# Token-ordered Strassen sums, weight splits in pieces, input sums on GpSimd and moved down products in a two-layer attention and SwiGLU kernel

## The chip, the cores and the metric

The kernel runs on one core of a Trainium2 chip. The metric is the device time of one execution in microseconds (us), as the median of several runs. A row of the profile such as "PE bank L335" names an engine (PE = TensorE, DVE = VectorE, ACT = ScalarE, POOL = GpSimd, SP = the queue that issues DMAs), the tile written and the line of the kernel.

## What is computed

Two layers, each an attention block with one key and value head and a SwiGLU block, over 2048 tokens of width 448, all in float32:

```python
def _A_ref(x, wq, wk, wv, wo):          # B, S, D, H = 1, 2048, 448, 16
    q = (x @ wq) in 16 heads of 28;  k = x @ wk;  v = x @ wv
    p = softmax(q k^T * 28 ** -0.5)
    return (p v, heads joined) @ wo
def _B_ref(x, w_gate, w_up, w_down):    # F = 1792
    return (silu(x @ w_gate) * (x @ w_up)) @ w_down
for _ in range(2):
    x = x + _A_ref(layernorm(x), A_wq, A_wk, A_wv, A_wo)
    x = x + _B_ref(layernorm(x), B_w_gate, B_w_up, B_w_down)
```

## The kernel before

Every matrix product with weights is done on numbers split in two: a high part, rounded to the short float format that TensorE takes at full rate, and a low part, the rest. A product is then three matmuls (high x high, high x low, low x high), or fewer where a row half is shared. `split` (L138) makes the two parts on GpSimd: one TENSOR_SCALAR for the high part (L139), one TENSOR_TENSOR for the low one (L140).

**The feed-forward layer**, which the change touches, works on 4 token chunks c of 512 and 14 columns blocks fc of 128. Two column blocks are a group gi (7 groups). Groups 0 and 6 are done in *units* (`unit`, L1044), one per chunk and column block: gate and up products of the chunk in two banks of PSUM, in two halves of the contraction (two `side_by_side` calls), `Silu` on ScalarE (L1081), the product with up on VectorE (L1082), its high part `hh` on ScalarE (L1083), its low part `hl` on VectorE (L1086). The down products of a unit, two steps, are kept in a list `pend` and run in the next unit: the first step between that unit's halves, the second after them. After the last column block of a group the four banks of down products are added to the residual `xres` (`accumulate`, L977: two directly on VectorE, L985, two by a copy to a staging tile on ScalarE, L988, and an add on GpSimd, L989).

**Groups 1 to 5** are done by Strassen's method: per column block and pair of chunks (p = 0, 1) one *block* (`block`, L805), 20 blocks per layer. Its operands are sums: `T` of the input (made once per pair by `mix`, L777, 18 instructions of 128x512 each) and `S` of the weights (`sums`, L794, GpSimd). Its seven products go to banks x, y, z, w (steps A1 to A4, S0 to S5), and sums of these make gate and up of both chunks:

- `s1` copies x to SBUF (ScalarE, L850); `u2`, `w5`, `u3`, `C12`, `C22`, `C21` add banks and SBUF tiles (VectorE, L851 to L856). The SBUF tiles `u_, w_, v_, s_` are parts of the tile xn.
- `silB` (ScalarE, L857), `mulB` (VectorE, L859), `hhB` (L864), `hlB` (L868) make the hidden part of chunk b, and `silA` (L858, it reads bank x and so ends its use), `mulA` (L860), `hhA`, `hlA` that of chunk a.
- E1, E2 are the down products of chunk b, F1, F2 those of chunk a, each in four further banks. `fE`, `fF` and `fX` to `gZ` are tiny copies of one column per bank (`between`, "seen", L342) on ScalarE: TensorE writes a bank from its other row half only after them.
- Of E's and F's four banks, two are added to `xres` on VectorE (Ea0, Ea1, L882) and two copied to staging tiles on ScalarE (Ec2, Ec3, L877) and added on GpSimd (Ep2, Ep3, L884). There are **two** staging buffers, so Fc2 needs Ep2 to be done.

Within one column of a PSUM bank the tokens stand by the way they were turned: position n*4 + t holds token n of tile t. `in_turn` (L131) is the view of such a bank as (t, n), at a stride of four words; `by_tile` (L135) is the plain order. In before, the sums stay in the bank's order, and `silB`, `mulB` and `mulA` put them in token order when they read.

What sets the order of the work is the table `ORDER` (L765): each engine gets the steps in that order; a name with one dash belongs to the block before, with two dashes to the one before that. `w1` and `w2` are places for weight work: `w1` splits the weights of the column block after next (`parted`, L173) and makes their sums, ahead of Ep2 in GpSimd's queue; `x1`, `x2`, `x3` are places where `mix` instructions that are left over (`extra`) go. Nothing reorders it afterwards; an engine waits in order.

Blocks of a group in order j = 0 to 3: (p 0, A), (p 0, B), (p 1, A), (p 1, B). At j = 0 GpSimd splits the weights of block column B (from the second such group on); at j = 1 it makes sums and splits (groups 1 to 4; group 5 splits only); at j = 3 it makes sums.

`rest` (L1146) begins the feed-forward layer: the norm of chunk 3 (its copies of 64 columns of xn are L246, on GpSimd), then the sums of the first weights, then the groups. The transposes of chunk 3 (L285) stand in the unit (0, 2, 1).

Of the kernel before, what the change touches and what calls it, by code (L numbers as in the profile page):

```python
# [52 lines left out]
def forward(  # L53
# [292 lines left out]
    class Attention:  # L346
# [418 lines left out]
    ORDER = (  # L765
        "A1 C21- Fc2-- Fp2-- mulA- A2 fY fX Fa0-- Fa1-- A3 fZ fW Fc3-- Fp3-- A4 s1 hhA- u2 x1 E1- w1 w5 fE- u3 S0 "
        "hlA- x2 gY E2- Ea0- Ea1- x3 Ec2- Ep2- Ec3- Ep3- w2 S1 gX S2 gZ S3 gW S4 F1- C12 C22 silB mulB fF- S5 hhB hlB F2- silA"
    ).split()

    class FeedForward:  # L770
        def __init__(self, layer):
            self.layer, self.X, self.W, self.norms = layer, {}, {}, {}
            self.pend, self.soon, self.dn, self.flip, self.mid, self.left = [], [], {}, 0, {}, []
            self.blocks, self.extra = [], []
            self.nxt = Attention(1) if layer == 0 else None

        def mix(self, p):  # L777
# [4 lines left out]
            t = qraw  # L782
            tt = nc.vector.tensor_tensor
            fs = []
            for i, *terms in ((2, b1[0], b0[0], b0[1], b1[1]), (0, b0[0], a0[0], a0[1], b0[1]), (1, b1[0], t, None, b1[1]), (3, a1[0], t, None, a1[1])):
                fs.append(lambda x=terms[0], y=terms[1]: tt(t, x, y, ALU.subtract))  # L786
# [3 lines left out]
                fs.append(lambda i=i: nc.vector.tensor_copy(hi[i], t))  # L790
                fs.append(lambda i=i: tt(lo[i], t, hi[i], ALU.subtract))
            return fs
# [12 lines left out]
        def block(self, p, fc):  # L805
# [43 lines left out]
            tt = nc.vector.tensor_tensor  # L849
            o["s1"] = lambda: nc.scalar.copy(s_, x)  # L850
            o["u2"] = lambda: tt(u_, y, s_, ALU.add)  # L851
            o["w5"] = lambda: tt(w_, z, u_, ALU.add)
            o["u3"] = lambda: tt(v_, w, u_, ALU.add)
            o["C12"] = lambda: tt(w_, y, w_, ALU.add)  # L854
            o["C22"] = lambda: tt(v_, z, v_, ALU.add)
            o["C21"] = lambda: tt(u_, w, u_, ALU.add)  # L856
            o["silB"] = lambda: nc.scalar.activation(by_tile(s_), in_turn(w_), AF.Silu)  # L857
            o["silA"] = lambda: nc.scalar.activation(by_tile(sg), in_turn(x), AF.Silu)  # L858
            o["mulB"] = lambda: tt(by_tile(s_), in_turn(v_), by_tile(s_), ALU.mult)  # L859
            o["mulA"] = lambda: tt(by_tile(sg), in_turn(u_), by_tile(sg), ALU.mult)  # L860

# [4 lines left out]
            for k, raw, e, c in (("B", s_, "E", b), ("A", sg, "F", a)):  # L866
# [12 lines left out]
                def add(e, c, t):  # L879
                    r = xres[:, 4 * c + t, :]  # L880
                    if t < 2:
                        tt(r, d[t][:, 0:D], r, ALU.add)  # L882
# [6 lines left out]
                for t in range(4):  # L889
                    o[f"{e}{'aapp'[t]}{t}"] = lambda e=e, c=c, t=t: add(e, c, t)  # L890
                for t in (2, 3):
# [17 lines left out]
        def blocked(self, gi):  # L909
# [25 lines left out]
            for j, (p, fc) in enumerate((p, fc) for p in range(2) for fc in (A, B)):  # L935
                for n, k in (("x1", 2), ("x2", 1), ("x3", 1)):
                    jobs[j][n] = [self.extra.pop(0) for _ in range(min(k, len(self.extra)))]
                self.blocks.append(self.block(p, fc))
                self.run(jobs[j])
            if last:  # L940
                o = self.blocks[-1]
                self.blocks.append({})
                f = [o.pop(k) for k in ("F1", "fF", "F2")]
                self.run({})
                self.pend = [lambda: (f[0](), f[1]()), f[2], o["Fa0"], lambda: [o[k]() for k in ("Fc2", "Fp2", "Fa1", "Fc3", "Fp3")]]
                part(A + 3)

        def down(self, fs, fc, d, hh, hl, w=None):


            dh, dl = w or self.W[fc][2:]
            self.flip = 1 - self.flip
            one, two = ((0, 1), (2, 3)) if self.flip else ((2, 3), (0, 1))
# [90 lines left out]
        def unit(self, gi, c, n):  # L1044
# [92 lines left out]
        def verdict(self, last):  # L1137
# [6 lines left out]
            nc.vector.tensor_reduce(whole, row[0:1, 0:P], AX.X, ALU.min)  # L1144

        def rest(self, xb):  # L1146
            self.stage = xb.enter_context(tc.tile_pool(name=f"stage{self.layer}", bufs=2, reuse_waits="tile"))
# [6 lines left out]
            for c in (2, 3):  # L1154
                self.X[c] = xtile(self.xbp, self.xd[c])
            cut(self.norms[2], self.X[2])
# [5 lines left out]
            mixing = ExitStack()  # L1162
            if mixed:
                pool = mixing.enter_context(tc.tile_pool(name=f"mix{self.layer}", bufs=1, reuse_waits="tile"))
                self.S = [(q[:, 0, :], q[:, 1, :]) for q in qts]
                self.S.append((kd.rearrange("p g n -> p (g n)"), pool.tile([P, 512], F32R, name="sums")))
                self.apart = pool.tile([P, 512], F32, name="apart")
                self.T = [keys, [pool.tile([P, 2, 512], F32R, name=f"mixed{i}") for i in range(4)]]
                self.sums(FG, columns(FG))
                self.extra += self.mix(0)  # L1170
            for gi, fs in enumerate(groups):
# [9 lines left out]
                for c in range(NC) if gi not in mixed else ():  # L1181
                    for n in range(len(fs)):
                        if mixed and (gi, c, n) == (0, 3, 0):
                            self.extra += self.mix(1)
# [88 lines left out]
```

## Time and profile before

| what | us |
|---|---|
| median of 3 runs (2034.92 to 2038.86) | 2035.11 |
| the profiled execution's own time | 2036.95 |
| its span, first to last instruction | 2035.2 |
| TensorE busy in it | 1980.6 |
| feed-forward, layer 0: first stretch 592 to 667 / blocks 667 to 950 / end and next projection 950 to 1060, TensorE busy | 63.12 of 75 / 276.99 of 283 / 104.03 of 110 |
| feed-forward, layer 1: 1604 to 1678 / 1678 to 1960 / 1960 to 2035, TensorE busy | 62.96 of 74 / 276.24 of 282 / 65.88 of 75 |
| both attention layers, TensorE busy | 588.33 of 592, 543.11 of 544 |
| VectorE, ScalarE, GpSimd busy over the span | 1130.9, 1371.1, 729.2 |

Read the table by stages: TensorE has almost no pause in attention, and some 12 us in each first stretch, 6 in the blocks of each layer and 6 to 9 at each end. A row of the timeline gives start, duration (us), engine, line, operation, out<-in, size, and in brackets the idle time of that engine before it and what ended it. x2 at the end of a row are two instructions put together.

### The profile page before, as it was taken

How to read it: one execution, taken by the hardware profiler on the slowest of the kernel's cores; microseconds unless marked ns; L12 is line 12 of the kernel's file. 1: busy time of each engine (PE TensorE's matmuls, PEld its weight loads, DVE VectorE, ACT ScalarE, POOL GpSimd, SP SyncE). 2: the span in 40 equal slices, each digit the busy share in tenths (PEclk: the TensorE clock that was granted, in tenths of full speed). 3: DMA queues.
4: the chain of work that ended last, by engine and by line, in shares of the span. 5: the costliest groups of instructions: out<-in, count | busy, mean ns of one | idle time of the engine just before them, and what ended most of it. 6: DMA issues, size and time to landing. Idle time of an engine off the chain costs nothing. (4 is left out here: it accounts for less than half of the span.)

```text
span 2035.2 us, 45408 instructions
## 1 busy us (share of the span) xinstructions
PE 1980.6 (97%) x18267; PEld 1291.2 (63%) x18267; DVE 1130.9 (56%) x1805; ACT 1371.1 (67%) x2417; POOL 729.2 (36%) x772
## 2 busy tenths in 40 slices
PE   9999999999998999999999999999999979999998
PEld 7544545445477788888884444454444868888887
DVE  7443544545457676775564335445454577677753
ACT  4899898998932444444348998989989334444532
POOL 4222111124124566664342221212231245667540
PEclk9999999999998999999999999999999989999999
DMA  5111110212110011100131111102111100111102
GB/s 163 50 30 30 30 43 12 61 38 58 34 37 16 16 31 31 30 21 17 55 99 39 29 30 30 43 12 60 52 45 34 37 16 16 31 31 31 31 1 74
DMA packets 95510, 78.62 MB, mean 39 GB/s; under 512 B 23582, under 2 KB 78494, under 8 KB 95294
## 3 DMA queue, kind: packets, MB, share of 16 engines
q1 hardware_dynamic: 95006, 75.21, 13.2%
q8 instruction: 144, 2.36, 0.5%
q14 instruction: 72, 0.59, 0.1%
q10 hardware_dynamic: 288, 0.46, 0.1%
HBM read 56.11 MB, written 18.74 MB: 37 GB/s over the span
## 5 line engine op out<-in xcount | busy, mean ns | idle before, releaser
L659 PE MATMUL bank<-pt,vsb 128*32 128x512 f32 x4096 | 493.3, 598 | 0.3
L618 PE MATMUL bank<-qstack,keys 32*128 32x512 f32 x1536 | 484.6, 425 | 0.0
L618 PE MATMUL three<-qstack,keys 32*128 32x512 f32 x4608 | 459.8, 425 | 1.5 <-DVE vt L552 1.2
L618 PEld LDWEIGHTS three<-qstack,keys 32*128 32x128 f32 x4608 | 254.0, 182 | 295.3 <-ACT pt L631 181.1
L625 ACT ACTIVATE pt<-three 128x1536 f32<-128x1536 f32 x256 | 372.2, 1454 | 0.6 <-ACT pt L631 0.3
L631 ACT ACTIVATE pt<-three 128x1536 f32<-128x1536 f32 x256 | 372.1, 1454 | 0.0
L335 PE MATMUL bank<-xh,wgh 64*128 64x512 f32 x1248 | 330.7, 399 | 17.5 <-ACT sg L858 16.3
L335 PE MATMUL bank<-wdh,h 64*128 64x448 f32 x1776 | 315.8, 373 | 9.2 <-ACT h L864 6.6
L627 DVE COPY raw<-bank 128x512 f32<-128x512 f32 x256 | 177.4, 693 | 226.4 <-PE bank L618 224.1
L669 DVE TENSOR_TENSOR o<-bank,o 128x512 f32<-128x512 f32 x224 | 154.9, 692 | 240.2 <-PE bank L659 235.6
L342 ACT COPY seen<-bank 128x1 f32<-128x1 f32 x820 | 103.2, 163 | 266.1 <-PE bank L335 261.6
L884 POOL TENSOR_TENSOR xres<-stage,xres 128x448 f32<-128x448 f32 x160 | 198.1, 1253 | 234.6 <-ACT stage L877 234.6
L335 PE MATMUL bank<-xh,wgl 64*128 64x512 f32 x924 | 265.7, 395 | 0.0
L659 PEld LDWEIGHTS bank<-pt,vsb 128*32 128x32 f32 x4096 | 107.1, 109 | 249.7 <-issue 152.6
L698 POOL TENSOR_TENSOR o<-o 128x512 f32<-128x512 f32 x32 | 41.2, 1288 | 587.3 <-DMA o<-rd 546.3
L618 PEld LDWEIGHTS bank<-qstack,keys 32*128 32x128 f32 x1536 | 243.4, 183 | 0.6 <-DVE o L669 0.3
L335 PE MATMUL bank<-xl,wgh 64*128 64x512 f32 x816 | 226.0, 398 | 0.0
L335 PEld LDWEIGHTS bank<-wdh,h 64*128 64x128 f32 x1776 | 196.0, 187 | 35.0 <-DVE xres L882 7.4
L335 PEld LDWEIGHTS bank<-xh,wgh 64*128 64x128 f32 x1248 | 168.0, 188 | 50.0 <-ACT sg L858 14.5
L630 ACT ACTIVATE pt<-bank 128x512 f32<-128x512 f32 x256 | 151.5, 592 | 59.5 <-PE bank L618 59.4
L335 PE MATMUL bank<-wdl,h 64*128 64x448 f32 x888 | 184.4, 371 | 0.0
L628 ACT ACTIVATE pt<-raw 128x512 f32<-128x512 f32 x256 | 159.3, 622 | 0.0
(201 smaller groups left out, 3159.3 us busy)
## 6 DMA issues: line engine op xcount, KB each, us to landing
o<-rd SPq DMA_DIRECT2D x32, 256.0 KB
qraw<-qd SPq DMA_DIRECT2D x128, 56.0 KB
qd<-stage SPq DMA_DIRECT2D x30, 224.0 KB
xt<-xn SPq DMA_DIRECT2D x28, 224.0 KB
wdr<-in_B_w_down_dram SPq DMA_DIRECT2D x28, 224.0 KB
wr<-in_B_w_gate_dram SPq DMA_DIRECT2D x30, 192.0 KB
wr<-in_B_w_up_dram SPq DMA_DIRECT2D x30, 192.0 KB
xn<-xt SPq DMA_DIRECT2D x7, 768.0 KB
```

The lines of the kernel that those rows point to most:

```text
L335: nc.tensor.matmul(po, a, b, start=start, stop=stop, skip_group_check=True)
L342: nc.scalar.copy(seen[:, i : i + 1], po[:, 0:1])
L618: nc.tensor.matmul(three[:, j, :] if j < 3 else one, k[js, kp, ks], q[js, part, :], start=(z == 0), stop=(z == 2), tile_position=(32 * j, 0),)
L625: nc.scalar.activation(pt, three, AF.Exp, scale=SCALE)
L627: nc.vector.tensor_copy(raw, one)
L628: nc.scalar.activation(pt1, raw, AF.Exp, scale=SCALE)
L630: nc.scalar.activation(pt1, one, AF.Exp, scale=SCALE)
L631: nc.scalar.activation(pt, three, AF.Exp, scale=SCALE)
L659: nc.tensor.matmul(po[32 * j : 32 * j + 32, :], vsb[:, n % NT, :], pts[n][j], start=(n == 2 * d), stop=(n > 2 * d), skip_group_check=True,)
L669: nc.vector.tensor_tensor(acc, in_turn(po), acc, ALU.add)
L698: nc.gpsimd.tensor_tensor(rb, oraw, rb, ALU.mult)
L884: nc.gpsimd.tensor_tensor(r, h[e, t], r, ALU.add)
```

## The change

1. *Order of the tokens.* `s1`, `u2`, `w5`, `u3`, `C12`, `C22`, `C21` read their bank through `in_turn` and write token order, so `silB`, `mulB` and `mulA` read and write plain tiles.
2. *Pieces.* `parted` calls `split` four times on [128, 256] and twice on [128, 224], instead of once on [128, 1024] and once on [128, 448].
3. *Input sums.* The first pair's `mix` runs on GpSimd, six instructions before the groups and four at the end of each unit until they are used up; the second pair's stays on VectorE, up to six per unit (five before), and `x1` goes from the table while `x3` takes two.
4. *The last block.* E's and F's down products of the last block leave the table. E's go into the first unit of group 6, F's into the second, the first step between the unit's halves each time; all eight banks are added on VectorE. The first unit's own down products move one unit on.
5. `down` no longer changes `flip` for blocks, so E and F begin with the same row halves; the staging-tile rule "t < 2" becomes "no staging copy was made".

```diff
-        split(h, l, r)
-        split(dh, dl, rd)
+        for k in range(4):
+            split(h[:, k], l[:, k], r[:, k])
+        for ns in (slice(0, 224), slice(224, D)):
+            split(dh[:, ns], dl[:, ns], rd[:, ns])
...
-        "A1 C21- Fc2-- Fp2-- mulA- A2 fY fX Fa0-- Fa1-- A3 fZ fW Fc3-- Fp3-- A4 s1 hhA- u2 x1 E1- w1 w5 fE- u3 S0 "
+        "A1 C21- Fc2-- Fp2-- mulA- A2 fY fX Fa0-- Fa1-- A3 fZ fW Fc3-- Fp3-- A4 s1 hhA- u2 E1- w1 w5 fE- u3 S0 "
         "hlA- x2 gY E2- Ea0- Ea1- x3 Ec2- Ep2- Ec3- Ep3- w2 S1 gX S2 gZ S3 gW S4 F1- C12 C22 silB mulB fF- S5 hhB hlB F2- silA"
...
-            o["s1"] = lambda: nc.scalar.copy(s_, x)
-            o["u2"] = lambda: tt(u_, y, s_, ALU.add)
...
-            o["C12"] = lambda: tt(w_, y, w_, ALU.add)
...
-            o["silB"] = lambda: nc.scalar.activation(by_tile(s_), in_turn(w_), AF.Silu)
+            plus = lambda out, po, r: tt(by_tile(out), in_turn(po), by_tile(r), ALU.add)
+            o["s1"] = lambda: nc.scalar.copy(by_tile(s_), in_turn(x))
+            o["u2"] = lambda: plus(u_, y, s_)
...
+            o["C12"] = lambda: plus(w_, y, w_)
...
+            o["silB"] = lambda: nc.scalar.activation(s_, w_, AF.Silu)
             o["silA"] = lambda: nc.scalar.activation(by_tile(sg), in_turn(x), AF.Silu)
-            o["mulB"] = lambda: tt(by_tile(s_), in_turn(v_), by_tile(s_), ALU.mult)
-            o["mulA"] = lambda: tt(by_tile(sg), in_turn(u_), by_tile(sg), ALU.mult)
+            o["mulB"] = lambda: tt(s_, v_, s_, ALU.mult)
+            o["mulA"] = lambda: tt(sg, u_, sg, ALU.mult)
...
-                for n, k in (("x1", 2), ("x2", 1), ("x3", 1)):
+                for n, k in (("x2", 1), ("x3", 2)):
...
-                f = [o.pop(k) for k in ("F1", "fF", "F2")]
+                ends = [[o.pop(e + k) for k in e_.split()] for e, e_ in (("E", "1 2 a0 a1 a2 a3"), ("F", "1 2 a0 a1 a2 a3"))]
...
-            for _ in range(min(5, len(self.extra))):
-                self.extra.pop(0)()
+            for fs_, k in ((self.more, 4), (self.extra, 6)):
+                for _ in range(min(k, len(fs_))):
+                    fs_.pop(0)()
...
+            if mixed:
+                self.sums(FG, columns(FG))
+                self.more = self.mix(0, nc.gpsimd, self.apart, lambda o, i: nc.gpsimd.tensor_scalar(o, i, 1.0, 0.0, ALU.mult, ALU.add))
+                for f in self.more[:6]:
+                    f()
+                del self.more[:6]
...
+                        if mixed and gi > mixed[-1] and c == 0:
+                            self.late, self.pend = (self.pend, self.late) if n == 0 else ([], self.late + self.pend)
```

Three places of the program show what this moves. First, GpSimd in a block that makes sums and splits (the weights' sums go from `apart` to kdiag and sums; `wr`, `wdr` are raw weights; `xres<-stage` are the adds Ep2, Ep3 and Fp2, Fp3). Before:

```order
L799 TENSOR_TENSOR apart<-wr 128x128
L800 TENSOR_TENSOR apart<-wr 128x128
L801 TENSOR_TENSOR apart<-apart,wr 128x128
L802 TENSOR_TENSOR apart<-wr,apart 128x128
L139 TENSOR_SCALAR qstack_101<-apart 128x512
L140 TENSOR_TENSOR qstack_101<-apart,qstack_101 128x512
L139 TENSOR_SCALAR wgh<-wr 128x1024
L140 TENSOR_TENSOR wgl<-wr,wgh 128x1024
L139 TENSOR_SCALAR wdh<-wdr 128x448
L140 TENSOR_TENSOR wdl<-wdr,wdh 128x448
L884 TENSOR_TENSOR xres<-stage,xres 128x448 x8
```

And the changed kernel from the split on:

```order
L139 TENSOR_SCALAR wgh<-wr 128x256
L140 TENSOR_TENSOR wgl<-wr,wgh 128x256
L139 TENSOR_SCALAR wgh<-wr 128x256
L140 TENSOR_TENSOR wgl<-wr,wgh 128x256
L139 TENSOR_SCALAR wgh<-wr 128x256
L140 TENSOR_TENSOR wgl<-wr,wgh 128x256
L139 TENSOR_SCALAR wgh<-wr 128x256
L140 TENSOR_TENSOR wgl<-wr,wgh 128x256
L139 TENSOR_SCALAR wdh<-wdr 128x224
L140 TENSOR_TENSOR wdl<-wdr,wdh 128x224
L139 TENSOR_SCALAR wdh<-wdr 128x224
L140 TENSOR_TENSOR wdl<-wdr,wdh 128x224
```

Four instructions become twelve in the same place, ahead of the same adds. Second, GpSimd in group 0, after the first weights' sums (`xn<-xn` are the copies for chunk 3, `xres<-stage` the adds of a chunk). Before:

```order
L139 TENSOR_SCALAR kdiag<-apart 128x512
L140 TENSOR_TENSOR sums<-apart,kdiag 128x512
L989 TENSOR_TENSOR xres<-stage,xres 128x448 x2
L246 COPY xn<-xn 128x64 x4
L989 TENSOR_TENSOR xres<-stage,xres 128x448 x4
```

In the changed kernel (`keys` are the tiles of the first pair's sums):

```order
L787 TENSOR_TENSOR apart<-xh 128x512
L789 TENSOR_TENSOR apart<-apart,xl 128x512
L790 TENSOR_TENSOR apart<-apart,xl 128x512
L1182 TENSOR_SCALAR keys_97<-apart 128x512
L792 TENSOR_TENSOR keys_97<-apart,keys_97 128x512
L787 TENSOR_TENSOR apart<-xh 128x512
L996 TENSOR_TENSOR xres<-stage,xres 128x448 x2
L789 TENSOR_TENSOR apart<-apart,xl 128x512
L790 TENSOR_TENSOR apart<-apart,xl 128x512
L1182 TENSOR_SCALAR keys_95<-apart 128x512
L792 TENSOR_TENSOR keys_95<-apart,keys_95 128x512
L248 COPY xn<-xn 128x64 x4
```

Ten of the eighteen `mix` instructions now stand ahead of the copies of xn. Third, VectorE at the end of the last block of layer 0 (sg is mulA or a unit's product, `h<-sg,h` is hlA or hl, `xres<-bank` are direct adds). Before:

```order
L860 TENSOR_TENSOR sg<-xn,sg 128x512
L882 TENSOR_TENSOR xres<-bank_7056,xres 128x448
L882 TENSOR_TENSOR xres<-bank_7057,xres 128x448
L868 TENSOR_TENSOR h_11521<-sg,h_11521 128x512
L882 TENSOR_TENSOR xres<-bank_7056,xres 128x448
L882 TENSOR_TENSOR xres<-bank_7057,xres 128x448
L1082 TENSOR_TENSOR sg<-bank_7052,sg 128x512
```

And in the changed kernel:

```order
L862 TENSOR_TENSOR sg<-xn,sg 128x512
L884 TENSOR_TENSOR xres<-bank_7080,xres 128x448
L884 TENSOR_TENSOR xres<-bank_7081,xres 128x448
L870 TENSOR_TENSOR h_11625<-sg,h_11625 128x512
L1089 TENSOR_TENSOR sg<-bank_7076,sg 128x512
L884 TENSOR_TENSOR xres<-bank_7080,xres 128x448
L1093 TENSOR_TENSOR h_11731<-sg,h_11731 128x512
L884 TENSOR_TENSOR xres<-bank_7081,xres 128x448
L884 TENSOR_TENSOR xres<-bank_78,xres 128x448
L884 TENSOR_TENSOR xres<-bank_79,xres 128x448
```

E's adds, four of them, now stand behind the first unit's product. On TensorE the first half of that unit stands ahead of E1, which followed F2 of the block before directly.

More of the change, by code (lines that the diff above doesn't have):

```diff
@@ L880, in add @@
                     r = xres[:, 4 * c + t, :]
-                    if t < 2:
+                    if (e, t) not in h:
                         tt(r, d[t][:, 0:D], r, ALU.add)
@@ L1144, in verdict, with lend @@
             nc.vector.tensor_reduce(whole, row[0:1, 0:P], AX.X, ALU.min)
+        def lend(self, mixing):
+            pool = mixing.enter_context(tc.tile_pool(name=f"mix{self.layer}", bufs=1, reuse_waits="tile"))
+            self.S = [(q[:, 0, :], q[:, 1, :]) for q in qts]
+            self.S.append((kd.rearrange("p g n -> p (g n)"), pool.tile([P, 512], F32R, name="sums")))
+            self.apart = pool.tile([P, 512], F32, name="apart")
+            self.T = [keys, [pool.tile([P, 2, 512], F32R, name=f"mixed{i}") for i in range(4)]]
         def rest(self, xb):
@@ L1160, in rest @@
             self.soon.append([1, lambda: [f() for f in third[5:]]])
-            self.mid[0, 2, 1] = [lambda ks=ks: self.turned(3, ks) for ks in ((0, 1), (2, 3))]
[L1162 to L1170, printed above, removed]
+            if mixed:
+                self.sums(FG, columns(FG))
[3 more added lines that the diff above has]
+                del self.more[:6]
+            self.mid[0, 2, 1] = [lambda ks=ks: self.turned(3, ks) for ks in ((0, 1), (2, 3))]
             for gi, fs in enumerate(groups):
```

32 lines of the change are left out of this document (19 added, 13 removed).

## The prediction

> **What bounds the kernel now.** TensorE works through nearly the whole span, so the first view to read is the one of waits, for TensorE alone: total, times, longest.
>
> ```profile
> PE bank L335 <- ACT sg L858: 16.3, 29, 3.4
> PE bank L335 <- DVE xn L851: 11.8, 2, 6.2
> PE bank L335 <- ACT h L864: 6.6, 2, 3.3
> PE bank L335 <- ACT stage L988: 1.4, 1, 1.4
> ```
>
> All four lie in the two feed-forward layers, and the change touches the work behind each. In order: A1 of a block waits for `silA` to leave bank x; S0 of the first Strassen block waits for `u2`; E1 of the last block waits for its banks; products wait for a copy that lacks a staging buffer. A fifth wait, for VectorE's `xl` in group 0, stands under term 4. The remaining time is matmuls, which the change neither adds nor removes.
>
> The timeline shows a wait's full price: start, duration, instruction, and in brackets the idle time.
>
> ```profile
> 772.45 0.37 PE L335 MATMUL bank<-wdh,h 64*128 64x448 f32 x2
> 773.08 0.46 PE L335 MATMUL bank<-xh,wgh 64*128 64x512 f32 x1 [0.25 <-ACT sg L858]
> ```
>
> Down products start 0.205 apart, so A1 could start at 772.66; it starts 0.42 later, though only 0.25 counts as idle. The same subtraction at the other block starts gives 0.31 to 0.45 at 29 boundaries, 0.12 at one, and about 1.08 at six. Those six are where GpSimd makes weight sums and splits weights in one block. The timeline of one of them, over all engines:
>
> ```profile
> 798.14 0.69 DVE L854 TENSOR_TENSOR xn<-bank,xn 128x512 f32<-128x512 f32 x1 [2.31 <-PE bank L335]
> 798.86 1.14 ACT L857 ACTIVATE xn<-xn 128x512 f32<-128x512 f32 x1 [1.70 <-DVE xn L854]
> 799.83 1.16 POOL L140 TENSOR_TENSOR wdl<-wdr,wdh 128x448 fp32r<-128x448 f32 x1
> 800.03 1.84 DVE L859 TENSOR_TENSOR xn<-xn 128x512 f32<-128x512 f32 x1 [0.60 <-ACT seen L342]
> 800.95 5.27 POOL L884 TENSOR_TENSOR xres<-stage,xres 128x448 f32<-128x448 f32 x3
> 801.90 0.62 ACT L864 CAST h<-xn 128x512 fp32r<-128x512 f32 x1 [1.68 <-DVE xn L859]
> 802.42 0.59 ACT L858 ACTIVATE sg<-bank 128x512 f32<-128x512 f32 x1
> 802.55 0.81 DVE L868 TENSOR_TENSOR h<-xn,h 128x512 fp32r<-128x512 f32 x1 [0.69 <-ACT h L864]
> 802.91 0.52 ACT L877 COPY stage<-bank 128x448 f32<-128x448 f32 x1
> 803.07 0.50 PE L335 MATMUL bank<-xh,wgh 64*128 64x512 f32 x1 [0.91 <-ACT sg L858]
> 804.14 0.35 ACT L342 COPY seen<-bank 128x1 f32<-128x1 f32 x2 [0.70 <-PE bank L335]
> ```
>
> Two things are to be seen. The chain into A1 is C12, silB, mulB, hhB, silA, one after another. And mulB, issued at 800.03 while GpSimd's `wdl` ran until 800.99, ended at 801.87, 0.88 after it: **a VectorE instruction with both inputs in SBUF waits out the GpSimd instruction that is running, and the next GpSimd instruction waits for it in turn**.
>
> **Term 1, token order, at the 30 ordinary boundaries.** The instructions by line, min/median/max in ns, then the page's row for a strided PSUM read:
>
> ```profile
> L857 ACT ACTIVATE xn<-xn x40: 1116/1127/1147, 663.1 to 1956.7; 128x512 f32<-128x512 f32 x40
> L859 DVE TENSOR_TENSOR xn<-xn x40: 1064/1083/1875, 664.3 to 1957.8; 128x512 f32<-128x512 f32 x40
> L868 DVE TENSOR_TENSOR h<-xn,h x40: 691/693/947, 666.9 to 1959.6; 128x512 fp32r<-128x512 f32 x40
> L669 DVE TENSOR_TENSOR o<-bank,o 128x512 f32<-128x512 f32 x224 | 154.9, 692 | 240.2 <-PE bank L659 235.6
> ```
>
> silB (L857) and mulB (L859) read SBUF at a stride of four words; afterwards they read it in order, as ScalarE's L864 (0.62 at 801.90) and VectorE's L868 do: 1.13 becomes 0.62, 1.08 becomes 0.69, 0.90 off the chain. The sums C12, u2 and the rest then read PSUM at that stride, as L669 does already in 0.692, what C12 takes now: no cost. Bounds: nothing saved if stride is not the reason, 0.90 if it is; I take 0.90, since the rows differ in nothing else. At most 0.45 of it shows, and TensorE is next to wait for nothing, so I leave 0.12 per boundary, the smallest seen. The 30 gaps sum to 11.2; 11.2 - 30 x 0.12 = **7.6 us**.
>
> **Term 2, the pieces, at the six heavy boundaries.** GpSimd's rows there:
>
> ```profile
> 793.38 0.94 POOL L139 TENSOR_SCALAR kdiag<-apart 128x512 fp32r<-128x512 f32 x1
> 794.41 1.30 POOL L140 TENSOR_TENSOR sums<-apart,kdiag 128x512 fp32r<-128x512 f32 x1
> 795.66 1.06 POOL L139 TENSOR_SCALAR wgh<-wr 128x1024 fp32r<-128x1024 f32 x1
> 796.80 2.41 POOL L140 TENSOR_TENSOR wgl<-wr,wgh 128x1024 fp32r<-128x1024 f32 x1
> 799.18 0.57 POOL L139 TENSOR_SCALAR wdh<-wdr 128x448 fp32r<-128x448 f32 x1
> ```
>
> From 1024 and 448 elements a line through two points gives 0.19 fixed for both kinds, 0.85 ns an element for TENSOR_SCALAR (1.06, 0.57), 2.17 for TENSOR_TENSOR (2.41, 1.16). Pieces of 256: 0.41 and 0.74; of 224: 0.38 and 0.67. Four pairs and two pairs, with the 0.08 between dependent rows and 0.03 overlap, are 6.9 against 5.3: **1.6 us later per set**, estimated. Smaller pieces let VectorE in more often, each time 0.55 to GpSimd: mulB, hlB and mulA all fall among them now.
>
> Queued behind the pieces is the add Ep2 (the first of the x3 at 800.95), which frees the staging buffer that Fc2, ScalarE's copy at 802.91, needs. Ep2 ended at about 802.87 (hlB, which waited for it, ended at 803.36): no slack was left. In the changed kernel the pieces start at 795.66 too: plus 6.9, plus three times 0.55, minus 0.4 where these fall into pauses, plus the add's 1.13, and Ep2 ends at 804.9. The next A1, freed by term 1, moves from 803.07 to 802.1. Behind Fc2 in ScalarE's queue stand the `seen` copies (804.14, ended 1.42 after A1) that A3 needs by A1 + 1.5 = 803.6. They end at 804.9 + 0.49 + 0.35 = 805.8: **a new wait of 2.2 at A3**. So each heavy boundary goes from 1.08 to 0.12 + 2.2: 1.24 worse, six times **-7.4 us**. Bounds: no new wait (gain 5.8 in all), and 0.5 more on each of the six TENSOR_SCALARs, as L139's 0.94 for 512 elements stands above the line's 0.62: rival 2. In blocks that only split, the 4.2 of weight sums ahead of the pieces are missing, Ep2 ends some 5 earlier, and I cost them at nothing; the cover is the 2 us that are left until Fc2 (with less, rival 2).
>
> **Term 3, the first blocks.** Before, `u2` waited behind five `mix` instructions of VectorE:
>
> ```profile
> 646.00 1.53 DVE L786 TENSOR_TENSOR qraw<-xh 128x512 f32<-128x512 f32 x1
> 653.15 0.68 DVE L851 TENSOR_TENSOR xn<-bank,xn 128x512 f32<-128x512 f32 x1
> 667.46 0.76 PE L335 MATMUL bank<-xh,wgh 64*128 64x512 f32 x1 [3.36 <-ACT sg L858]
> 1678.37 0.46 PE L335 MATMUL bank<-xh,wgh 64*128 64x512 f32 x1 [2.71 <-ACT sg L858]
> 1680.23 0.62 PE L335 MATMUL bank<-xh,wgh 64*128 64x512 f32 x1
> ```
>
> Five took 7.15, each waiting out one split instruction. Now six stand there, but they alternate with pieces: about 0.5 own and 0.55 of a piece each, 6.1 in all, starting 0.4 later because the unit before has a sixth too: `u2` comes 0.65 earlier. Two layers, **1.3 us**, bounds -1.5 to +2 each (contention as now; no contention). At 667.46 and 1678.37, the second blocks' A1, the 0.90 of term 1 comes off, plus an estimated 0.6 to 0.8 less waiting of mulB, which meets pieces there and no longer whole split instructions: **3.2 us**.
>
> A long wait costs more than its idle time, as the end of the last block shows:
>
> ```profile
> 949.78 0.37 PE L335 MATMUL bank<-wdh,h 64*128 64x448 f32 x2
> 958.78 0.63 PE L335 MATMUL bank<-xh,wgh 64*128 64x512 f32 x2
> 959.21 0.63 PE L335 MATMUL bank<-xl,wgh 64*128 64x512 f32 x2
> 959.97 0.39 PE L335 MATMUL bank<-xh,wgh 64*128 64x512 f32 x2
> 960.20 0.39 PE L335 MATMUL bank<-xl,wgh 64*128 64x512 f32 x1
> ```
>
> After a wait, pairs start 0.43 apart for some 4 us, then 0.23: about 1.9 lost. A1's wait at 667.46 falls to about 1.7, where this should mostly stay out: two times 1.9 x 0.6 = **2.2 us**. The Trainium skill, page "TensorE: Matmul & The Clock Gate", section "What's actually happening", lets the clock halve after an idle window of about 3.4 us. By that rule term 2's waits never cool TensorE; here the 2.71 was followed by slow rows (0.62 at 1680.23), so cooling stays a rival.
>
> **Term 4, first pair's sums on GpSimd.**
>
> ```profile
> 605.49 2.92 POOL L989 TENSOR_TENSOR xres<-stage,xres 128x448 f32<-128x448 f32 x2
> 609.85 2.63 POOL L246 COPY xn<-xn 128x64 f32<-128x64 f32 x4 [1.45 <-DVE xn L244]
> 621.99 1.97 PE L285 MATMUL bank<-ident,xn 128*128 128x128 f32 x8 [2.76 <-DVE xl L298]
> ```
>
> The transposes at 621.99 waited because VectorE had `mix` in front of `xl`. That goes. Next late is POOL's COPY of `xn`, which the last four transposes read: ten `mix` instructions and two adds now stand ahead of it. The sums ended at 605.49; without `mix` on VectorE, some 0.9 earlier. From 604.6: six (1.30 each, a copy 0.62) to 612.5, adds to 615, four to 619.8, copies to 621 to 622, with 1 us of lock waits in it. The four transposes follow at 622 instead of about 623: gain 1 to 2, **3 us** over both layers; bounds 0 to 3.5 each. The Trainium skill, page "GPSIMD Engine Reference", section "8. Key points", calls VectorE about twice as fast for elementwise work: by it the 14 two-input steps cost 14 x (1.30 - 0.69) = 8.5 more per layer. It does not change the sum, which already has the steps at GpSimd's price: only what passes 619.2, when TensorE is ready, is paid. The last eight steps and two adds follow in some 12 us, with two whole units still ahead of the first block, which reads them.
>
> **Term 5, the end of the last block.**
>
> ```profile
> 952.69 1.13 DVE L882 TENSOR_TENSOR xres<-bank,xres 128x448 f32<-128x448 f32 x2
> ```
>
> From 949.99 (949.78 + 0.205) to 958.78 stand twelve pairs of products, 2.46: 6.3 lost, plus 0.6 of slow pairs. E1 waited for these adds (VectorE was in mulA). Now eleven pairs of the next unit's gates, 2.5, stand ahead of E1, and F's products lie between halves too. What is late next: C21 holds the unit's bank 0.4; F1 waits for four direct adds 0.9; `seen` after the second unit's first step, behind `hh` in ScalarE's queue, 0.6; small ones 0.5. 6.9 - 2.4 = 4.5, two layers **9 us**, bounds 2.5 to 6 each. The waits for `stage` (L988, layer 0) go since F no longer uses staging: 1.4 idle, **2 us** with restart.
>
> **Sum.** 7.6 - 7.4 + 1.3 + 3.2 + 2.2 + 3 + 9 + 2 = 20.9. The profiled execution took 2036.95, 1.84 above the median of the runs: 2016.0 there, **2014 us** as median.
>
> **Rivals.** (1) *The pieces cost no wait*: Ep2 in time, each heavy boundary 0.12: 7.4 + 5.8 more, 2001. For it: shorter locks. Against it: no slack at 802.91. (2) *GpSimd becomes the bound of the split blocks*: at the slow TENSOR_SCALAR price a set takes 3 us more; the heavy waits rise to about 5, and cool TensorE (1.9): +4.7 six times; the eight split-only boundaries get mulB and C21 behind pieces, about 1.3 each. 2014 + 28 + 10 = 2052. It decides for slower from 1.7 us more per set; at 1 us more it is near 2034. (3) *The new waits cool TensorE*: six times 1.9, 2025. (4) *Stride is not the reason*: A1 stays at 803.07, so term 1 is missing, A3's wait is 1.2, and term 3 gives 2 instead of 5.4: 0 - 7.2 + 1.3 + 2 + 3 + 9 + 2 = 10.1, again 2025. (5) *GpSimd is late in group 0* (term 4 at its lower bound and below) costs 3 to 5 and stays inside the range.
>
> **Chances.** Forecast (2006 to 2021) 0.42; rival 1, 0.22; rivals 3 and 4 (2021 to 2031), 0.19; rival 2 begun (2031 to 2039), 0.08; rival 2 in full, 0.09. A measurement tells apart about 0.2%, 4 us. So faster 0.83, same 0.08, slower 0.09. The range leaves out rival 2 in full, half of it begun, and the end below rival 1: 1998 to 2034.
>
> **What would show it.** silB near 0.62, mulB near 0.69. PE's wait for `sg` nearly gone; in its place six waits for `seen` of about 2 us, 3 us into POOL's adds. `u2` near 5.6 idle. No 3.3 us wait after the last F2. The sum is wrong if GpSimd's sets take over 8 us, or if A1 still waits at ordinary boundaries.

## The result, and the profile after

| | us |
|---|---|
| before, median of 4 runs (2034.92 to 2038.86) | 2035.24 |
| changed, median of 4 runs (2003.78 to 2007.69) | 2005.95 |
| ratio, 95% interval | 0.9852 (0.9835 to 0.9869) |
| profiled execution of the changed kernel: its own time / span | 2007.16 / 2005.4 |

The forecast was 2014, 21 us faster; it became 29 us faster. The waits of TensorE, total, times and longest, without the rows of other stages (line numbers of the changed kernel are two higher than before at the blocks, and more further down):

```profile
PE bank L337 <- ACT seen L344: 12.5, 8, 2.6
PE bank L337 <- DVE xn L851: 8.1, 3, 4.1
PE bank L337 <- ACT sg L860: 3.9, 2, 2.1
PE bank L337 <- DVE sg L1089: 1.8, 2, 1.2
PE bank L337 <- DVE xres L884: 0.9, 2, 0.7
PE bank L287 <- POOL xn L248: 0.9, 2, 0.5
```

A1's wait for `sg` is left in 2 places of 29, at A1 of the second block in each layer. The waits for `h` (E1 of the last block, 6.6 before) and for `stage` are gone; the transposes' wait fell from 5.5 to 0.9. In their place stands a new first row, the wait for `seen`, as forecast for the six heavy boundaries.

To see what each part is worth, cut the span at the starts of the same matmuls in both profiled executions (blocks counted 0 to 19 per layer; a period runs from one block's A1 to the next):

| stretch, both layers together | before | changed | gain | forecast |
|---|---|---|---|---|
| group 0 up to the unit behind the transposes | 62.92 | 57.87 | 5.1 | 3 |
| that unit to A1 of block 0 | 40.14 | 38.54 | 1.6 | 0 |
| A1 of block 0 to A1 of block 2 | 79.32 | 72.07 | 7.2 | 6.7 and two of term 1's boundaries |
| 28 ordinary periods from block 2 on | 410.4 | 392.9 | 17.5 | 7.1 (28 of 30) |
| 6 heavy periods | 91.9 | 104.6 | -12.7 | -7.4 |
| last block's A1 to the next projection or the last matmul | 171.3 | 158.5 | 12.8 | 11 |
| the rest | | | -1.7 | 0 |

The sum is 29.8, the difference of the spans. (The long period ends at a heavy A1 in the kernel before, and begins at it in the changed one.) Two rows are far from the forecast, in opposite directions: the ordinary periods and the heavy ones.

An ordinary boundary now looks like this on TensorE (start, duration, instruction):

```profile
690.06 0.56 PE L337 MATMUL bank<-wdl,h 64*128 64x448 f32 x2
690.27 0.55 PE L337 MATMUL bank<-wdh,h 64*128 64x448 f32 x2
690.47 0.39 PE L337 MATMUL bank<-xh,wgh 64*128 64x512 f32 x1
```

The last down products start at 690.27, A1 0.20 later: the gap, 0.42 at 773.08 before, is 0.00, here and at every other block from block 2 on. The period is 14.00 us, where 14.66 was usual. The reason stands in the lines by duration, min/median/max in ns:

```profile
L859 ACT ACTIVATE xn<-xn x40: 632/634/635, 658.8 to 1930.1; 128x512 f32<-128x512 f32 x40
L861 DVE TENSOR_TENSOR xn<-xn x40: 691/693/1142, 659.5 to 1930.8; 128x512 f32<-128x512 f32 x40
```

silB went from 1127 to 634, mulB from 1083 to 693: the stride had been their whole excess, as term 1 took it.

A heavy boundary, over all engines:

```profile
726.46 0.41 POOL L139 TENSOR_SCALAR wgh<-wr 128x256 fp32r<-128x256 f32 x1
726.95 0.74 POOL L140 TENSOR_TENSOR wgl<-wr,wgh 128x256 fp32r<-128x256 f32 x1
731.71 0.60 ACT L860 ACTIVATE sg<-bank 128x512 f32<-128x512 f32 x1
732.59 0.39 PE L337 MATMUL bank<-xh,wgh 64*128 64x512 f32 x1
733.44 0.99 POOL L140 TENSOR_TENSOR wdl<-wdr,wdh 128x224 fp32r<-128x224 f32 x1
734.38 4.46 POOL L886 TENSOR_TENSOR xres<-stage,xres 128x448 f32<-128x448 f32 x4
735.57 0.53 ACT L879 COPY stage<-bank 128x448 f32<-128x448 f32 x1 [3.26 <-POOL xres L886]
736.00 0.74 ACT L344 COPY seen<-bank 128x1 f32<-128x1 f32 x4
736.22 0.51 PE L337 MATMUL bank<-mixed,qstack 64*128 64x512 f32 x1 [1.92 <-ACT seen L344]
738.66 0.90 PE L337 MATMUL bank<-wdh,h 64*128 64x448 f32 x2
740.30 0.54 PE L337 MATMUL bank<-wdh,h 64*128 64x448 f32 x2
```

Follow the chain from the top. The pieces take from 726.46 to 734.43, 8.0 us. Only then comes Ep2, the first of four adds at 734.38. Fc2, which needs the staging buffer that Ep2 frees, starts at 735.57 after ScalarE sat idle for 3.26; the `seen` copies follow; A3 starts at 736.22, idle for 1.92. That is the forecast chain link by link: it put A3 at A1 + 3.7, and it came at A1 + 3.63. What the forecast left out of its sum, and kept as rival 3, is below the wait: the pairs behind it run slowly (0.90 for two down products at 738.66, 0.54 for the same at 740.30).

### The profile page after: what moved, and what is told of

It reads as the page before. It is cut to its first block, busy times and chain, and to the rows that moved or that the text cites. A ratio compares the mean times of both kernels' runs of the same rounds, so it can differ in the third digit from the quotient of the medians.

```text
span 2005.4 us, 45589 instructions
## 1 busy us (share of the span) xinstructions
PE 1965.1 (98%) x18267; PEld 1334.2 (67%) x18267; DVE 1067.9 (53%) x1777; ACT 1357.2 (68%) x2409; POOL 803.7 (40%) x1024
## 5 line engine op out<-in xcount | busy, mean ns | idle before, releaser
L337 PE MATMUL bank<-xh,wgh 64*128 64x512 f32 x1248 | 359.4, 395 | 5.3 <-ACT sg L860 3.9
L337 PE MATMUL bank<-wdh,h 64*128 64x448 f32 x1776 | 344.3, 368 | 1.6 <-DVE xres L884 0.9
L337 PE MATMUL bank<-xh,wgl 64*128 64x512 f32 x924 | 283.3, 393 | 0.0
L337 PEld LDWEIGHTS bank<-wdh,h 64*128 64x128 f32 x1776 | 261.0, 187 | 12.6 <-DVE xres L884 2.5
L886 POOL TENSOR_TENSOR xres<-stage,xres 128x448 f32<-128x448 f32 x152 | 190.2, 1267 | 177.0 <-ACT stage L879 177.0
L337 PE MATMUL bank<-xl,wgh 64*128 64x512 f32 x816 | 247.1, 394 | 0.0
L337 PE MATMUL bank<-wdl,h 64*128 64x448 f32 x888 | 229.5, 371 | 0.0
L851 DVE TENSOR_TENSOR xn<-bank,xn 128x512 f32<-128x512 f32 x240 | 158.0, 686 | 131.9 <-PE bank L337 85.9
L337 PEld LDWEIGHTS bank<-xh,wgh 64*128 64x128 f32 x1248 | 201.6, 186 | 15.8 <-issue 3.5
```

The lines of the kernel that those rows point to most:

```text
L337: nc.tensor.matmul(po, a, b, start=start, stop=stop, skip_group_check=True)
L851: plus = lambda out, po, r: tt(by_tile(out), in_turn(po), by_tile(r), ALU.add)
L886: nc.gpsimd.tensor_tensor(r, h[e, t], r, ALU.add)
```

## The experiments

All times are medians; the ratio is to runs of the kernel before on the same chip.

### Each part alone

Token order alone: the kernel before with part 1 of the change (the `plus` lines, and silB, mulB, mulA on plain tiles).

> The kernel before with the token order alone. Theory (the two traces compared): the stride was what made silB and mulB long, so both fall to about 0.63 and 0.69; the ordinary blocks' period falls from 14.66 to 14.0 (30 boundaries, about 18 us), the whole splits leave at most a short wait at A3 (heavy blocks 14.7 instead of 15.3, 4 us), the second blocks' A1 comes 0.9 earlier: about 2011 us. The prediction's own sizes for the same edit (7.6 + 2 + 3) would give 2022. Rival, stride is not the reason: silB stays near 1.13, time 2035.

Measured 2001.77 us, ratio 0.9816 (0.9802 to 0.9829): this part alone is faster than the whole change.

```profile
L858 ACT ACTIVATE xn<-xn x40: 632/633/636, 663.3 to 1926.0; 128x512 f32<-128x512 f32 x40
PE bank L335 <- ACT sg L859: 3.5, 2, 1.7
PE bank L335 <- ACT h L865: 2.8, 2, 1.4
```

silB is at 633, and A1's wait has gone from 29 places to 2. Ordinary periods are 13.98 to 14.09, the six heavy ones 14.35 to 14.41. The rival is out. The 9 us beyond the expected 2011 are mostly (7.0) at the end of each layer: E1 of the last block waits 1.4 instead of 3.3, and the stretch from the last A1 on is 84.0 and 80.3 instead of 87.5 and 83.8. The edit brings VectorE to its adds sooner there: in layer 0 the two direct adds of that place (L882, L883 here) begin at 936.66, 1.15 after the last down products ahead of E1 (935.51), where they began 2.9 after them (952.69 and 949.78).

Pieces alone:

```diff
-        split(h, l, r)
-        split(dh, dl, rd)
+        for k in range(4):
+            split(h[:, k], l[:, k], r[:, k])
+        for ns in (slice(0, 224), slice(224, D)):
+            split(dh[:, ns], dl[:, ns], rd[:, ns])
```

> The kernel before with the splits in pieces alone. Theory (Ep2 stands behind the pieces and holds a staging buffer): A3 waits for the seen copies at the six heavy boundaries, about 1.5 us each, while mulB is locked out 0.3 us less; the first blocks gain some 3 us in all: 2035 to 2042 us, more if the waits are followed by slow products. Rival, smaller pieces only shorten locks: no wait for seen, faster than before, about 2029.

Measured 2053.92 us, ratio 1.0085 (1.0071 to 1.0098): 17 us slower, worse than the theory's 7.

```profile
PE bank L337 <- ACT sg L860: 21.0, 28, 2.8
PE bank L337 <- ACT seen L344: 11.8, 8, 1.9
```

The waits for `seen` are there, 1.86 each at the six heavy boundaries. The two periods on the sides of such an A1 were 15.3 and 14.5, and are 14.8 and 16.7 to 18.3: 15 in all. The term that the theory missed is the first row, which grew from 16.3 to 21.0: in the blocks that only split, mulB falls among the pieces, A1's gap is 1.3 to 1.4 instead of 0.42, and nine such periods rose from 14.66 to about 15.6, 8.5 in all. The first blocks gave some 6 back.

First pair's input sums on GpSimd alone (`mix` with an engine, `more`, six and four at a time):

> The kernel before with the first pair's input sums on GpSimd alone. Theory: the transposes' wait for xl goes (5 us over both layers, by the trace of the changed kernel), u2 of the first block gains nothing, since its mix instructions still wait out whole splits and there is one more: about 2030 to 2032 us. Rival, GpSimd is late in group 0 and the transposes wait for xn instead: 2035.

Measured 2032.02 us, ratio 0.9978 (0.9968 to 0.9989). The stretch of group 0 up to the unit behind the transposes fell from 31.79 to 28.94 in layer 0, as in the changed kernel; `u2` gained nothing (its wait is 6.4 at the longest, 6.2 before). Both parts of the theory held.

Last block's down products alone (with the constant row halves, part 5):

> The kernel before with the last block's down products moved alone (and the row halves kept). Theory: the stretch from the last block's A1 to the end of each feed-forward layer falls as in the changed kernel, 8.6 and 3.6 us: about 2023 us. Rival, the gain of that stretch came from the earlier parts (shorter mulA and silB ahead of it): 2029 or more.

Measured 2021.15 us, ratio 0.9916 (0.9903 to 0.993). Somewhat more than expected, and the trace shows a reason that has nothing to do with the last block: ordinary periods are 14.41 to 14.55 (one 14.78), not 14.66.

### The row halves

So the line on the row halves was tried by itself:

```diff
-            self.flip = 1 - self.flip
+            self.flip = self.flip if w else 1 - self.flip
```

> The kernel before with one line changed: the blocks' down products all begin with the same row halves. Theory (from the kernel with the last block moved, which has this line too: its ordinary blocks take 14.51 us, not 14.69): E1's weight loads wait for the direct adds in 8 places and no longer in 25, so the 38 block periods lose some 0.15 each: 2030 us. Rival, the last block's move is what shortened them: 2035 to 2036, ordinary blocks 14.69.

Measured 2032.74 us, ratio 0.9992 (0.998 to 1.0003): not to be told from no change. But the ordinary periods are 14.39 to 14.55 (one 14.81), so the theory is right for the blocks. The view of waits for TensorE's weight loads shows it, first of the kernel before, then of this one:

```profile
PEld bank L335 <- DVE xres L882: 7.4, 25, 0.3
```

```profile
PEld bank L335 <- DVE xres L882: 5.8, 8, 2.4
```

In the kernel before, E1's first weights wait for the direct adds of the block before in 25 places, some 0.3 each. With constant halves this is gone from the ordinary blocks (4.5 us over both layers, from A1 of block 2 to A1 of block 19: 249.0 and 248.7, before 251.2 and 251.1). What is left are two waits of 2.1 at E1 of the last block, and `stage` is waited for 2.8 where it was 1.4: from the last A1 on, the layers take 87.7 and 86.1, before 87.5 and 83.8, so that 2.5 is given back. With the last block moved these waits are gone.

### What the pieces cost in the changed kernel

Whole splits back, all else as changed (the diff of the pieces, turned round):

> The changed kernel with the whole splits of before put back, all else as changed. Theory (the pieces hold Ep2, and with it the staging buffer, the seen copies and A3): heavy blocks fall from 17.2 us on average to 14.4, as in the kernel with the token order alone, 17 us; the mix instructions ahead of the first u2 meet whole splits again and lose some 3: about 1990 us. Rival, GpSimd's input sums or the moved last block cause part of the long waits: heavy blocks stay above 15, time over 1996.

Measured 1989.0 us, ratio 0.9769 (0.9753 to 0.9785): 17 us faster than the changed kernel (by the two ratios), the waits for `seen` down to 0.4 in 2 places. Heavy periods are 14.37 to 14.40, one 14.86.

```profile
PE bank L335 <- ACT seen L342: 0.4, 2, 0.2
```

The same pieces, behind Ep2 and Ep3:

```diff
-                {"w1": [lambda: sums(A + 2), lambda: part(A + 2)], "w2": [lambda: fetch(A + 3)]},
+                {"w1": [lambda: sums(A + 2)], "w2": [lambda: part(A + 2), lambda: fetch(A + 3)]},
```

> The changed kernel with the pieces kept, but in the heavy blocks issued behind Ep2 and Ep3 instead of ahead of them; GpSimd has the same work in each block. Theory (what matters is what stands ahead of Ep2): the waits for seen at A3 go, heavy blocks 14.0 to 14.4, 1986 us. Rival, GpSimd has too much work in that block (16.6 us of it in 14), whatever its order: the wait moves to the next block's staging copies, 2000 us or more.

Measured 1985.26 us, ratio 0.974 (0.9726 to 0.9753). Its waits:

```profile
PE bank L337 <- DVE xn L851: 8.0, 3, 4.1
PE bank L337 <- ACT sg L860: 3.4, 2, 1.7
PE bank L1231 <- POOL ident masks.py:199: 1.9, 1, 1.9
PE bank L337 <- DVE sg L1089: 1.8, 2, 1.2
```

The wait for `seen` is 0.4 in 2 places, none of them at A3, and every block from block 2 on takes 13.97 to 14.14. GpSimd does exactly the same instructions in the same block; two adds have changed places with twelve pieces. The sets of pieces in these blocks take as long as in the changed kernel, 7.96 to 8.36 (there 7.95 to 8.33). So neither the amount of GpSimd's work nor the contention of pieces with VectorE makes the 1.9 us waits by itself: it is what stands ahead of Ep2.

The split moved one block on, where GpSimd had only its adds:

```diff
-                {"w1": [lambda: sums(A + 2), lambda: part(A + 2)], "w2": [lambda: fetch(A + 3)]},
-                {},
+                {"w1": [lambda: sums(A + 2)]},
+                {"w1": [lambda: part(A + 2)], "w2": [lambda: fetch(A + 3)]},
```

> The changed kernel with the pieces kept, but the split of the next group's first column (and the load behind it) moved from the block that also makes sums to the next one, where GpSimd had only its adds. Both theories expect the waits for seen to go: 1985 us. If the waits came from the pieces' contention with VectorE and not from the queue ahead of Ep2, they stay: 2000 us.

Measured 1983.37 us, ratio 0.9734 (0.9721 to 0.9747); no wait for `seen` at A3 (0.4 in 2 places elsewhere), periods 13.98 to 14.15. And with whole splits at the same place:

> As the one before, with whole splits in place of pieces: heavy blocks 14.0, the first blocks some 3 us slower than with pieces: 1987 us. If pieces are worse than whole splits even where nothing waits in their queue, this is the faster of the two by more than 4.

Measured 1987.21 us, ratio 0.9748 (0.9735 to 0.9762). The intervals of the last three kernels overlap; what can be said is that pieces are not worse than whole splits once nothing that TensorE needs stands behind them.

### Where the 0.66 per ordinary period came from

Token order took 0.66 off a period, A1's gap was only 0.37 on average (11.2 over 30). To see whether the shorter mulA was the rest, it alone got its stride back, in the kernel with the token order alone (chunk a's tokens then stand in another order, so this kernel does the same work but computes something else):

```diff
-            o["mulA"] = lambda: tt(sg, u_, sg, ALU.mult)
+            o["mulA"] = lambda: tt(by_tile(sg), in_turn(u_), by_tile(sg), ALU.mult)
```

> The kernel with the token order alone, but with mulA reading and writing at the old stride of four words (its tokens are then permuted, so chunk a's hidden part is another than the reference's). Theory: a long mulA (1.6 us) pushes the two direct adds Fa0 and Fa1 back, and the next block's E1 waits for them again, about 0.11 us and as much of restart: ordinary blocks 14.1 to 14.2 us instead of 14.0, 2002 + 38 x 0.15, some 2007 us; A1 still waits for nothing. Rival, the 0.24 per block beyond A1's gap was only TensorE's restart after A1's wait: ordinary blocks stay at 14.0, time 2002.

Measured 2006.95 us, ratio 0.9854 (0.9837 to 0.9871). The number is the theory's, but the blocks don't bear it out. Most ordinary periods are still 13.99 to 14.07; only the first ones of layer 0 are 14.14 to 14.34, and the heavy ones are 14.33 to 14.52. VectorE's mulA in a block of each kind:

```profile
710.98 1.97 DVE L861 TENSOR_TENSOR sg<-xn,sg 128x512 f32<-128x512 f32 x1
712.88 1.13 DVE L883 TENSOR_TENSOR xres<-bank,xres 128x448 f32<-128x448 f32 x2
713.53 0.19 PEld L335 LDWEIGHTS bank<-wdh,h 64*128 64x128 f32 x2 [0.31 <-DVE xres L883]
838.22 1.08 DVE L861 TENSOR_TENSOR sg<-xn,sg 128x512 f32<-128x512 f32 x1
839.23 1.14 DVE L883 TENSOR_TENSOR xres<-bank,xres 128x448 f32<-128x448 f32 x2
```

Stride alone makes mulA 1.08; where it took 1.97 it also waited out a GpSimd instruction, the adds came late, and E1's weights waited 0.31. At 838.22 the adds are done at 840.37, and E1's first weights load at 840.52 without a wait. So the link from the direct adds to E1 is shown, but a strided mulA is not enough to close it. In the kernel before, mulA's median is 1592 ns, against 1078 here; that the longer chain silB, mulB, hlB, C21 ahead of it made it late there, so that it met GpSimd's add, is argued from the rows and was not tried apart. The trace has 2.3 us of the 5.2 (spans 2001.7 and 2004.0), 1.3 of it in the periods from block 3 on; the rest lies in the spread of the runs, and stays open.

### A version that goes on from there

The split moved on, and the second pair's input sums taken off VectorE's last unit ahead of the first block:

```diff
-            for fs_, k in ((self.more, 4), (self.extra, 6)):
+            for fs_, k in ((self.more, 4), (self.extra, 6 if n == 0 else 0)):
...
-                for n, k in (("x2", 1), ("x3", 2)):
+                for n, k in (("x2", 3), ("x3", 3)):
```

> The changed kernel with the first column's split moved to the free block, and with the second pair's input sums taken off VectorE's last unit: they go behind the first blocks' own sums, three at x2 and three at x3. Theory: u2 of the first block stands behind no mix instruction, its wait of 4.1 and 3.4 us falls under 0.5, and the slow products after it go: 1974 us. Rival, the sums moved into the blocks delay E's direct adds and the T of the second pair, and the waits come back there: 1983.

Measured 1978.31 us, ratio 0.9709 (0.9694 to 0.9723), the fastest of all: 28 us under the changed kernel, and 5 under the version with only the split moved on (1983.37), whose interval just touches this one's.

```profile
PE bank L337 <- ACT sg L860: 6.7, 2, 3.6
PE bank L337 <- DVE sg L1089: 1.7, 2, 1.2
```

The wait for `u2` is gone (8.0 before), as the theory said, but A1 of the second block waits 3.6 and 3.1 instead of 1.7 and 2.0: 3.0 of the 8.0 came back one block later. There C12, and silB, mulB and hlB after it, now stand behind six `mix` instructions of VectorE. The time lies between the theory's 1974 and the rival's 1983.

## Why the prediction was right, and where it was off

**Direction and mechanism** held: the parts that had a term did what it said, and the new wait came at the place, by the chain and nearly with the length that term 2 gave. The sum was 8.4 us short, from errors of 10 and 5 us that partly cancel and several small ones; that it came this near is in part luck. The time of 2005.95 lies at the edge of the band 2006 to 2021, not far from rival 1's 2001, but not by rival 1's mechanism: the new waits came.

**Term 1** (7.6 forecast, 17.5 in 28 periods) was mis-sized in three ways. Gaps were priced down to 0.12 each, "the smallest seen", and went to 0.00: with A1's other inputs ready, nothing was next late (3.6 over 30). A restart (slow products behind a wait) was left out: of the 0.66 that a usual period lost, 0.42 is the gap and 0.15 what the row halves alone take off; about 0.09 is left for it. And the weight loads' wait for the direct adds was not read at all, because the view of waits was asked for TensorE's matmuls alone; it was 7.4 us in 25 places, a row of the same view for weight loads.

**The row halves** (part 5) were not priced. Alone they shorten the periods by 0.15 and lose half of it at the ends. In the changed kernel this overlaps with token order, which removes the same wait by itself.

**Term 2** (-7.4 forecast, -12.7 measured): Ep2 was forecast to end at A1 + 2.8, Fc2 started at A1 + 2.98; the wait was forecast at 2.2 and is 1.84 to 2.62. The sets of pieces take 7.95 to 7.98 at five of the six boundaries and 8.33 at the one with the longest wait; 8 had been named as a sign that the sum is wrong, but 6.9 and VectorE's turns, as written, already give 8.15. Off was the price of what follows. Rival 3, that the waits cool TensorE, had been kept apart at a small chance; it happened at four of the six boundaries, whose periods are 17.8 and 17.9. The other two are 16.25 and 17.00.

**Term 3** (6.7 forecast, 7.2 measured with two ordinary boundaries in it): the total is near, its shares are not. `u2`'s wait fell to 4.08 and 3.39 instead of 5.6 (six times 0.5 and 0.55 are 6.3 and not the 6.1 that was written, so its own figures gave a smaller gain still), the second blocks' A1 to 1.80 and 2.10 instead of some 1.7 and 1.1. By the granted clock, TensorE worked 4.1 us less at half speed in these stretches, worth some 2.1, as forecast. Two new waits of 0.54 and 0.59 took part of it back.

**Term 4** (3 forecast, 5.1 measured): the copies of xn were finished at 621.55 in layer 0, as forecast; but TensorE, which came to the last four transposes at 620.66, waited for them 0.43 only. The 1.6 of the next row of the table fits the price of the old wait: the granted clock of the kernel before was 0.50 for 3.41 us behind it in each layer (from 621.92 and from 1635.68), and in the changed kernel it is not.

```profile
620.80 0.75 POOL L248 COPY xn<-xn 128x64 f32<-128x64 f32 x4
621.09 0.85 PE L287 MATMUL bank<-ident,xn 128*128 128x128 f32 x4 [0.43 <-POOL xn L248]
```

**Term 5** (11 forecast, 12.8 measured): of the small waits listed as next late, only the direct adds' 0.75 and the seen copies' 0.2 appear in layer 0. The view puts E1's old wait down to `h`, the prediction to the direct adds. The rows bear the prediction out:

```profile
952.79 0.62 ACT L864 CAST h<-sg 128x512 fp32r<-128x512 f32 x1 [1.67 <-DVE sg L860]
953.40 0.32 PEld L335 LDWEIGHTS bank<-wdh,h 64*128 64x128 f32 x2 [3.63 <-ACT h L864]
```

E1's first weights load at 953.40, just before that copy ends at 953.41 and 0.11 after the first direct add ends at 953.29.

**Rival 1** (pieces cost no wait) fell with the heavy boundaries. **Rival 2** (GpSimd becomes the bound of the split blocks) fell in the changed kernel, where the periods that only split are 14.1, but with the pieces alone its second half happened: nine boundaries that only split lost some 0.9 each, where it priced eight at 1.3. There mulB takes 2.00 to 2.05 among the pieces; in the changed kernel it meets them too, but takes 1.08 to 1.14, and no boundary waits. So that loss exists, and token order covers it. Its first half, heavy waits of 5, came nowhere (1.9 with the pieces alone), so that 2053.92 lies near its 2052 is chance. **Rival 4** (stride is not the reason) fell with silB's 634 ns.

The parts alone give 0.9816, 0.9916, 0.9978 and 1.0085, which would multiply to 0.979; together they gave 0.9852. Token order and the last block's move each remove E1's waits and shorten the last stretch (by 7.0 and 11.5 alone, by 12.8 in the changed kernel), and that counts once.

## What to carry to other kernels

Before cutting a piece of work finer on an engine that isn't the bound, look at what stands behind it in that engine's queue and who waits for that: here twelve pieces ahead of two adds cost 17 us, and the same pieces behind the adds nothing that could be seen. When a wait is taken away, read all views of the bounding engine (its matmuls and its weight loads) for what else was late by as much, and price the restart as well as the idle time. Try the parts of a change apart: here one of four cost 17 us, about half of the 35 that another one brought.

## What the hardware showed beyond that

The slow pairs after a wait keep to a clock of their own. In the profile of the changed kernel, waits of nearly the same length were followed by slow pairs or not:

```profile
796.14 0.50 PE L337 MATMUL bank<-mixed,qstack 64*128 64x512 f32 x1 [1.90 <-ACT seen L344]
854.48 0.50 PE L337 MATMUL bank<-mixed,kdiag 64*128 64x512 f32 x1 [1.84 <-ACT seen L344]
```

The granted clock of the profile tells them apart. A row has a stretch of the span, its length, TensorE's busy time in it with the number of matmuls, the granted clock as a share of full speed, and the DMA engines' busy share and GB/s:

```profile
733.19:736.60 3.41, 1.49 (x13) 1.00 0.61 176
736.60:740.01 3.41, 3.41 (x19) 0.50 0.08 25
794.63:798.04 3.41, 1.90 (x16) 1.00 0.37 111
798.04:801.45 3.41, 3.41 (x34) 1.00 0.01 5
852.65:856.07 3.42, 1.59 (x13) 1.00 0.50 138
856.07:859.48 3.41, 3.41 (x22) 0.50 0.05 15
1845.93:1849.35 3.42, 1.85 (x17) 1.00 0.44 128
1849.35:1852.76 3.41, 2.36 (x21) 1.00 0.29 93
1852.76:1856.17 3.41, 3.41 (x35) 1.00 0.00 0
```

At the heavy boundaries the clock was halved four times, for 3.41 us each, from 736.60, 856.07, 1729.88 and 1791.32. These starts are 35, 256 and 18 times 3.413 us apart: they lie on one grid, and each slow stretch is one step of it. The four waits that were followed by one lie inside the step ahead of it and fill 53 to 56% of it, so a slow stretch can begin up to 1.6 us after its wait has ended. The wait before 796.14 lies across a grid line, 0.4 and 1.5 us on its sides, and so does the longest one, 2.62 before 1850.40, with 1.6 and 1.1; no step is idle for half of its length, and no slow stretch follows.

The profiles of all thirteen kernels of this case, whose grids lie differently, bear this out. From 590 us on, steps at full clock that TensorE left idle for less than 45% (1781 of them) were never followed by a slow one; of those idle for 45 to 55%, 20 of 39 were; of those above, all 63. The kernel with the pieces alone shows it at the same waits of 1.9: three of its six heavy periods are 18.3, and just these have a slow step; the other three are 16.7 to 16.8. No experiment set the phase on purpose, and what decides between 45 and 55% is open.

The Trainium skill, page "TensorE: Matmul & The Clock Gate", section "What's actually happening", states a free-running activity window of 3.413 us, and the trace agrees with its length and that it runs free. It lets the clock fall after a whole idle window; here 1.84 us within one window were enough, and the measurement decides. The price of one slow window is about 1.6 us: the periods of 17.8 stand against 16.25 at the same wait. The prediction's 1.9 for some 4 us is near that, but slow stretches come in whole steps: the one that it read at 958.78 was two steps long, from 953.02 to 959.84.

If the grid lies differently from run to run, as it does between the profiles, a kernel with waits of this length has a time that depends on the phase. Twelve runs of the kernel with the row halves alone, which has many of them, lie between 2026.22 and 2038.42 with mean granted clocks of 0.991 and 0.986 at the ends; five runs of the kernel with the pieces behind the adds lie between 1984.2 and 1985.62. That the phase is the cause of this spread is argued, not shown.
